# The gate's activations of a recurrence with a highway layer: u stored as pairs of tokens and transposed as 32-bit words

## The chip, the cores and the metric

The kernel runs on one core of a Trainium2 chip. The metric is the device time of one execution in microseconds, of which the median over several runs is given. The times of the profile come from one profiled execution; its span goes from the first to the last instruction.

## What is computed

The input is x and f_logit, both 4 x 6336 x 256 in float32, a lower bound and a bias of 256 values each, and two matrices of 256 x 256. The first half is a recurrence over the 6336 tokens of each of four batches, the second a highway layer on its output:

```python
sig = 1.0 / (1.0 + np.exp(-f_logit))
f = lower_bound + (1.0 - lower_bound) * sig
i = 1.0 - f
for t in range(S):
    h = f[:, t] * h + i[:, t] * x[:, t]
    y[:, t] = h
H = np.maximum(y @ w_h, 0.0)
T = 1.0 / (1.0 + np.exp(-(y @ w_t + b_t)))
out = T * H + (1.0 - T) * y
```

## The kernel before

The 25344 tokens are cut into 29 units. A full unit has 1024 tokens of one batch: partition p of 128 holds 8 neighbouring tokens (nb = 8) with their 256 channels. Three units at the start and three at the end are shorter (2 or 4 tokens a partition), and one has 6 tokens a partition from four batches. A unit goes through these stages, each a function whose letter stands in the order:

- l and x load f_logit and x (tokens on the partitions), on the SP queue.
- u (L240) is one ScalarE instruction: u = sigmoid(-f_logit), which is 1 - sig, stored as f16 in the tile `u`.
- b (L246) multiplies u with x, two tokens of each partition in one instruction, on GpSimd or, where the order says v, on VectorE. The result `bv` is bf16 and is stored as pairs: the values of two neighbouring tokens lie side by side for each channel.
- i (L255) transposes u on TensorE, for one half h of the channels, to channels on the partitions: one transpose of 128 x 128 f16 for each of the nb tokens. It goes into one PSUM bank, `uT`, where the tokens then lie sorted by j, the place of a token within its partition.
- f (L263) computes f = 1 - (1 - lower_bound) u from uT, on ScalarE or (v) VectorE. It reads uT in steps, so that the tokens come in their order, and stores f16 in order.
- p (L279) transposes bv, for one half of the channels, with one f32 transpose for each pair of tokens: two bf16 values make one 32-bit word. The words are written in steps of nb/2 words, so that `bT` has the tokens in order.
- s (L301) is the recurrence, one scan on VectorE along the tokens, from f and bT to `y`, with the last column of the unit before as its start.
- z and g (L312) are the two matrix products, t (L328) the sigmoid of z on ScalarE, d (L333) the maximum with g on VectorE, E and e (L339) the product of d and t on GpSimd and VectorE.
- o (L350) brings tokens back to the partitions on TensorE (`op`), c (L365) copies it to SBUF on ScalarE, and w stores it through SP.

The channel factor 1 - lower_bound, by which b leaves out a part of i, is multiplied into the weights and into `diag` once at the start.

The order of all of this is a list written out in the kernel (L72 to L123); each word is a stage with its unit, its half and, behind a colon, its PSUM slot. uT and bT share two slots of one bank each (a0 and a1), and z, g and op share three slots of two banks (b0 to b2). Every instruction is pinned to the order of the list on its engine. The helper `shared` (L209) makes a product on GpSimd wait for the product on VectorE ahead of it in the list.

Of the kernel before, what the change touches and what calls it, by code (L numbers as in the profile page):

```python
# [11 lines left out]
FP32 = mybir.dt.float32  # L12
BF16 = mybir.dt.bfloat16
FP16 = mybir.dt.float16
AF = mybir.ActivationFunctionType
# [4 lines left out]
def kernel(  # L20
# [10 lines left out]
    nc = tc.nc  # L31
    B, S, D = x.shape
    assert (B, S, D) == (4, 6336, 256)
    P = 128
    NH = D // P
    NB = 8
# [3 lines left out]
    units = [  # L40
        (0, 128, 2, 0, 'y', 4, 0),
        (0, 128, 2, 256, 'y', 4, 0),
        (0, 128, 4, 512, 'y', 4, 0),
        (0, 128, 8, 1024, 'y', 4, 1280),
        (0, 128, 8, 2048, 'y', 4, 2048),
        (0, 128, 8, 3072, 'y', 4, 0),
        (0, 128, 8, 4096, 'y', 4, 2048),
        (0, 128, 8, 5120, 'yk', 4, 0),
# [81 lines left out]
    st = [dict() for _ in range(NU)]  # L130
    pin = tc.keep_in_program_order

    def sb(shape, dtype, name):
        return pool.tile(shape, dtype, tag=name, name=name, bufs=bufs.get(name, 1))

    def one_bank(slot, dtype, name):
        return ps.tile([P, NB * P], dtype, tag=f"a{slot}", name=name)
# [7 lines left out]
    ident_h = sb([P, P], FP16, "ident_h")  # L145
    make_identity(nc, ident_h)
    ident_f = sb([P, P], FP32, "ident_f")
# [21 lines left out]
    def tokens(n):  # L169
        return units[n][1] * units[n][2]  # L170
# [38 lines left out]
    def shared(ins, gpsimd):  # L209

        if not gpsimd:
            held[:] = [ins]
        elif held:
            tc.add_manual_dep(ins.ins, held.pop().ins.name, mybir.DependencyInfo(
                mybir.DependencyClass.Sync, mybir.DependencyReason.DATA), reason="shared port")
# [23 lines left out]

    def do_u(n, k, eng, slot):  # L240
        np_, nb = units[n][1:3]
        u = sb([P, NB, D], FP16, "u")
        pin(nc.scalar.activation(u[:np_, :nb], st[n]["l"][:np_, :nb], AF.Sigmoid, scale=-1.0))  # L243
        st[n]["u"] = u

    def do_b(n, k, eng, slot):  # L246
        np_ = units[n][1]
        if "bv" not in st[n]:
            st[n]["bv"] = sb([P, NB // 2, D, 2], BF16, "bv")
        q = 2 * k  # L250
        e = nc.vector if eng else nc.gpsimd
        shared(pin(e.tensor_mul(st[n]["bv"][:np_, k].rearrange("p d j -> p j d"), st[n]["u"][:np_, q:q + 2],  # L252
                                st[n]["x"][:np_, q:q + 2])), not eng)

    def do_i(n, h, eng, slot):  # L255
        np_, nb = units[n][1:3]
        uT = one_bank(slot, FP16, "uT")
        for j in range(nb):
            pin(nc.tensor.transpose(uT[:, j * np_:(j + 1) * np_], st[n]["u"][:np_, j, h * P:(h + 1) * P],  # L259
                                    ident_h[:np_, :np_]))  # L260
        st[n]["uT", h] = uT

    def do_f(n, h, eng, slot):  # L263
        N, nb = tokens(n), units[n][2]
        f = sb([P, NB * P], FP16, "f")
        to, of = f[:, :N], st[n]["uT", h][:, :N]
        if isinstance(units[n][0], int):
            to = to.rearrange("c (p j) -> c p j", j=nb)
            of = of.rearrange("c (j p) -> c p j", j=nb)
        else:  # L270
            to = to.rearrange("c (b p j) -> c b p j", b=B, j=nb)
            of = of.rearrange("c (j p b) -> c b p j", b=B, j=nb)
        if eng:
            pin(nc.vector.tensor_scalar(to, of, ncc[:, h:h + 1], 1.0, op0=ALU.mult, op1=ALU.add))
        else:
            pin(nc.scalar.activation(to, of, AF.Identity, scale=ncc[:, h:h + 1], bias=1.0))  # L276
        st[n]["f", h] = f

    def do_p(n, h, eng, slot):  # L279
        np_, nb = units[n][1:3]  # L280
        bT = one_bank(slot, BF16, "bT")
        words = bT.bitcast(FP32)
        g = nb // 2
        for k in range(g):
            pair = st[n]["bv"][:np_, k, h * P:(h + 1) * P].rearrange("p d j -> p (d j)").bitcast(FP32)
            if isinstance(units[n][0], int):
                to = words[:, k:k + g * (np_ - 1) + 1:g]
            else:
                to = words[:, :g * np_].rearrange("c (b p k) -> c p b k", b=B, k=g)[:, :, :, k]
            pin(nc.tensor.transpose(to, pair, ident_f[:np_, :np_]))  # L290
        st[n]["bT", h] = bT

    carry = {}
# [88 lines left out]
    for token in order.split():  # L382
# [5 lines left out]
        n, _, k = name[1:].partition(".")  # L388
# [29 lines left out]
```

## Time and profile before

| | |
|---|---|
| runs of the kernel, device us | 218.88 median of 3 (216.72 to 220.64) |
| span of the profiled execution | 215.2 us |
| TensorE (PE) busy | 190.1 us, 88% |
| VectorE (DVE) busy | 199.2 us, 93% |
| ScalarE (ACT) busy | 195.9 us, 91% |
| GpSimd (POOL) busy | 178.9 us, 83% |
| granted TensorE clock | 0.999 |
| moved by DMA | 78.69 MB, 366 GB/s in the mean |

The profiled execution has no device time of its own on record, only its span; the runs are 1.5 to 5.4 us longer than that span, which counts from the first instruction to the last. PE is the line of the matmuls and PEld that of the weight loads, which overlap them. A group of the profile gives the line, the engine, the operation, the tiles (result <- inputs) with partitions x elements and type, the count, the busy time in us and the mean of one in ns, and then the idle time of the engine just before them with what ended it.

### The profile page before, as it was taken

How to read it: one execution, taken by the hardware profiler on the slowest of the kernel's cores; microseconds unless marked ns; L12 is line 12 of the kernel's file. 1: busy time of each engine (PE TensorE's matmuls, PEld its weight loads, DVE VectorE, ACT ScalarE, POOL GpSimd, SP SyncE). 2: the span in 40 equal slices, each digit the busy share in tenths (PEclk: the TensorE clock that was granted, in tenths of full speed). 3: DMA queues.
4: the chain of work that ended last, by engine and by line, in shares of the span. 5: the costliest groups of instructions: out<-in, count | busy, mean ns of one | idle time of the engine just before them, and what ended most of it. 6: DMA issues, size and time to landing. Idle time of an engine off the chain costs nothing. (4 is left out here: it accounts for less than half of the span.)

```text
span 215.2 us, 4648 instructions
## 1 busy us (share of the span) xinstructions
PE 190.1 (88%) x1784; PEld 132.4 (62%) x1811; DVE 199.2 (93%) x164; ACT 195.9 (91%) x195; POOL 178.9 (83%) x166
## 2 busy tenths in 40 slices
PE   7477778988999799999998999999899999999881
PEld 3144456655766666675676766667676576776661
DVE  2789998999999899999998999999999999999960
ACT  4579889999999999999999999999999999999772
POOL 3045789997999999899998999887988999898910
PEclk9999999999999999999999999999999999999999
DMA  6999999999999999999999799998999999498275
GB/s 185 395 420 417 423 419 410 423 316 315 429 416 425 411 426 393 350 411 414 428 425 416 324 329 326 431 399 287 330 412 420 419 422 420 165 321 360 110 285 200
DMA packets 16750, 78.69 MB, mean 366 GB/s; under 512 B 2004, under 2 KB 2776, under 8 KB 11096
## 3 DMA queue, kind: packets, MB, share of 16 engines
q1 hardware_dynamic: 16720, 78.39, 92.7%
q8 instruction: 14, 0.23, 0.4%
q14 instruction: 8, 0.07, 0.1%
q10 hardware_dynamic: 8, 0.00, 0.0%
HBM read 52.43 MB, written 25.95 MB: 364 GB/s over the span
## 5 line engine op out<-in xcount | busy, mean ns | idle before, releaser
L252 POOL TENSOR_TENSOR bv<-u,x 128x512 bf16<-128x512 f16 x95 | 112.8, 1217 | 21.7 <-DVE w_sb L197 9.0
L307 DVE TENSOR_TENSOR_SCAN y<-f,y,bT 128x1024 bf16<-128x1024 f16 (+2 forms) x46 | 92.8, 2032 | 1.6 <-ACT f L276 0.9
L342 POOL TENSOR_TENSOR e<-d,t 128x512 bf16<-128x512 bf16 (+1 forms) x60 | 67.7, 1148 | 3.9 <-DVE e L342 3.0
L336 DVE SCALAR_TENSOR_TENSOR d<-y,ncc,g 128x1024 bf16<-128x1024 bf16 (+2 forms) x54 | 58.9, 1101 | 2.4 <-PE g L318 2.3
L331 ACT ACTIVATE t<-z,bt 128x1024 bf16<-128x1024 f32 (+3 forms) x58 | 57.9, 1019 | 2.0 <-PE z L318 1.3
L276 ACT ACTIVATE f<-uT,ncc 128x1024 f16<-128x1024 f16 (+3 forms) x53 | 55.4, 1057 | 4.2 <-PE uT L259 2.8
L318 PEld LDWEIGHTS <-w_sb 128*128 128x128 f16 x416 | 39.3, 99 | 32.2 <-issue 2.7
L372 ACT COPY o<-op 128x1024 f32<-128x1024 f32 (+2 forms) x53 | 51.2, 983 | 4.7 <-PE op L362 3.1
L243 ACT ACTIVATE u<-l 128x2048 f16<-128x2048 f32 (+3 forms) x29 | 49.2, 1695 | 3.8 <-DMA l<-in_f_logit_dram 3.6
L362 PE MATMUL op<-ident_b,e 128*128 128x128 bf16 x396 | 49.4, 219 | 1.0 <-DVE e L342 0.8
L318 PE MATMUL z<-y,w_sb 128*128 128x512 bf16 (+1 forms) x179 | 47.5, 372 | 1.2 <-DVE d L336 0.2
L318 PE MATMUL g<-y,w_sb 128*128 128x512 bf16 (+1 forms) x181 | 47.9, 372 | 0.7
L362 PEld LDWEIGHTS <-e 128*128 128x128 bf16 x396 | 44.0, 113 | 5.7 <-issue 2.2
L361 PE MATMUL op<-diag,y 128*128 128x128 f16 x368 | 45.9, 219 | 1.6 <-ACT o L372 0.9
L361 PEld LDWEIGHTS <-y 128*128 128x128 bf16 x368 | 41.0, 113 | 1.9
L290 PE MATMUL bT<-ident_f,bv 128*128 128x128 f32 x198 | 33.6, 283 | 7.2 <-POOL bv L252 2.5
L259 PE MATMUL uT<-ident_h,u 128*128 128x128 f16 x396 | 31.9, 221 | 7.7 <-DVE y L307 2.5
L259 PEld LDWEIGHTS <-u 128*128 128x128 f16 x396 | 26.6, 99 | 18.5 <-issue 7.9
L290 PEld LDWEIGHTS bT<-ident_f,bv 128*128 128x128 f32 x198 | 23.1, 142 | 17.0 <-POOL bv L252 3.8
L342 DVE TENSOR_TENSOR e<-d,t 128x512 bf16<-128x512 bf16 (+5 forms) x19 | 17.7, 943 | 1.0 <-PE op L362 0.7
L307 DVE TENSOR_TENSOR_SCAN y<-f,yr,bT 128x1024 bf16<-128x1024 f16 x4 | 9.3, 2333 | 0.0
L252 DVE TENSOR_TENSOR bv<-u,x 128x512 bf16<-128x512 f16 x4 | 3.4, 855 | 3.1 <-DMA x<-in_x_dram 3.1
(42 smaller groups left out, 48.9 us busy)
## 6 DMA issues: line engine op xcount, KB each, us to landing
out_dram<-o SPq DMA_DIRECT2D x46, 512.0 KB, 7.7
l<-in_f_logit_dram SPq DMA_DIRECT2D x22, 1024.0 KB, 11.1
x<-in_x_dram SPq DMA_DIRECT2D x22, 1024.0 KB, 13.8
l<-in_f_logit_dram SPq DMA_DIRECT2D x4, 256.0 KB, 8.7
x<-in_x_dram SPq DMA_DIRECT2D x4, 256.0 KB, 4.5
l<-in_f_logit_dram SPq DMA_DIRECT2D x2, 512.0 KB, 9.7
x<-in_x_dram SPq DMA_DIRECT2D x2, 512.0 KB, 7.5
out_dram<-o SPq DMA_DIRECT2D x3, 256.0 KB, 13.9
```

The source lines that it names most:

```text
L252: shared(pin(e.tensor_mul(st[n]["bv"][:np_, k].rearrange("p d j -> p j d"), st[n]["u"][:np_, q:q + 2], st[n]["x"][:np_, q:q + 2])), not eng)
L259: pin(nc.tensor.transpose(uT[:, j * np_:(j + 1) * np_], st[n]["u"][:np_, j, h * P:(h + 1) * P], ident_h[:np_, :np_]))
L276: pin(nc.scalar.activation(to, of, AF.Identity, scale=ncc[:, h:h + 1], bias=1.0))
L290: pin(nc.tensor.transpose(to, pair, ident_f[:np_, :np_]))
L307: pin(nc.vector.tensor_tensor_scan(y[:, c0:c0 + ln], st[n]["f", h][:, c0:c0 + ln], st[n]["bT", h][:, c0:c0 + ln], 0.0 if prev is None else ...
L318: pin(nc.tensor.matmul(p[:, a:e], w_sb[:, k, ki, m * P:(m + 1) * P], half(n, "y", ki)[:, a:e], start=ki == 0, stop=ki == NH - 1))
L331: pin(nc.scalar.activation(half(n, "t", m), st[n]["z", m][:, :tokens(n)], AF.Sigmoid, bias=bt[:, m:m + 1]))
L336: pin(nc.vector.scalar_tensor_tensor(half(n, "d", m), half(n, "y", m), ncc[:, m:m + 1], st[n]["g", m][:, :tokens(n)], op0=ALU.mult, op1=AL ...
L342: shared(pin(eng.tensor_mul(st[n]["e"][:, a:e], st[n]["d"][:, a:e], st[n]["t"][:, a:e])), eng is nc.gpsimd)
L361: pin(nc.tensor.matmul(o, half(n, "y", h)[:, cols], diag[:, h], start=True, stop=False))
L362: pin(nc.tensor.matmul(o, half(n, "e", h)[:, cols], ident_b, start=False, stop=True))
L372: pin(nc.scalar.copy(o[:np_, :w], st[n]["op", q][:np_, :w]))
```

## The change

The tile u gets the layout of bv: for each pair k of neighbouring tokens and each channel d, the two values lie side by side. ScalarE's one instruction for u stays one instruction and stores each f16 value 4 bytes from the one before it. The product b reads u in that layout. The stage i uses what p did: one f32 transpose for each pair of tokens and half, written in steps into the bank, through a common function `pairs`; p calls the same function. Then uT has the tokens in order, and f reads it in order, without the rearranged view. The list of the order, the slots, the tiles' sizes and the counts of instructions on ScalarE, VectorE, GpSimd and SP stay as they are; the transposes of u become half as many.

```diff
     def do_u(n, k, eng, slot):
         np_, nb = units[n][1:3]
-        u = sb([P, NB, D], FP16, "u")
-        pin(nc.scalar.activation(u[:np_, :nb], st[n]["l"][:np_, :nb], AF.Sigmoid, scale=-1.0))
+        u = sb([P, NB // 2, D, 2], FP16, "u")
+        pin(nc.scalar.activation(u[:np_, :nb // 2].rearrange("p k d j -> p k j d"),
+                                 st[n]["l"][:np_, :nb].rearrange("p (k j) d -> p k j d", j=2), AF.Sigmoid, scale=-1.0))
...
-        shared(pin(e.tensor_mul(st[n]["bv"][:np_, k].rearrange("p d j -> p j d"), st[n]["u"][:np_, q:q + 2],
-                                st[n]["x"][:np_, q:q + 2])), not eng)
+        shared(pin(e.tensor_mul(st[n]["bv"][:np_, k].rearrange("p d j -> p j d"),
+                                st[n]["u"][:np_, k].rearrange("p d j -> p j d"), st[n]["x"][:np_, q:q + 2])), not eng)
+
+    def pairs(n, src, h, words):
+        np_, g = units[n][1], units[n][2] // 2
+        for k in range(g):
+            pair = src[:np_, k, h * P:(h + 1) * P].rearrange("p d j -> p (d j)").bitcast(FP32)
+            if isinstance(units[n][0], int):
+                to = words[:, k:k + g * (np_ - 1) + 1:g]
+            else:
+                to = words[:, :g * np_].rearrange("c (b p k) -> c p b k", b=B, k=g)[:, :, :, k]
+            pin(nc.tensor.transpose(to, pair, ident_f[:np_, :np_]))
...
     def do_i(n, h, eng, slot):
-        np_, nb = units[n][1:3]
         uT = one_bank(slot, FP16, "uT")
-        for j in range(nb):
-            pin(nc.tensor.transpose(uT[:, j * np_:(j + 1) * np_], st[n]["u"][:np_, j, h * P:(h + 1) * P],
-                                    ident_h[:np_, :np_]))
+        pairs(n, st[n]["u"], h, uT.bitcast(FP32))
         st[n]["uT", h] = uT
...
         to, of = f[:, :N], st[n]["uT", h][:, :N]
-        if isinstance(units[n][0], int):
-            to = to.rearrange("c (p j) -> c p j", j=nb)
-            of = of.rearrange("c (j p) -> c p j", j=nb)
-        else:
-            to = to.rearrange("c (b p j) -> c b p j", b=B, j=nb)
-            of = of.rearrange("c (j p b) -> c b p j", b=B, j=nb)
...
     def do_p(n, h, eng, slot):
...
+        pairs(n, st[n]["bv"], h, bT.bitcast(FP32))
         st[n]["bT", h] = bT
```

More of the change, by code (lines that the diff above doesn't have):

```diff
@@ L251, in do_b @@
         e = nc.vector if eng else nc.gpsimd
-        shared(pin(e.tensor_mul(st[n]["bv"][:np_, k].rearrange("p d j -> p j d"), st[n]["u"][:np_, q:q + 2],
-                                st[n]["x"][:np_, q:q + 2])), not eng)
+        shared(pin(e.tensor_mul(st[n]["bv"][:np_, k].rearrange("p d j -> p j d"),
[9 more added lines that the diff above has]
+            pin(nc.tensor.transpose(to, pair, ident_f[:np_, :np_]))
     def do_i(n, h, eng, slot):
-        np_, nb = units[n][1:3]
         uT = one_bank(slot, FP16, "uT")
-        for j in range(nb):
-            pin(nc.tensor.transpose(uT[:, j * np_:(j + 1) * np_], st[n]["u"][:np_, j, h * P:(h + 1) * P],
-                                    ident_h[:np_, :np_]))
+        pairs(n, st[n]["u"], h, uT.bitcast(FP32))
         st[n]["uT", h] = uT
     def do_f(n, h, eng, slot):
-        N, nb = tokens(n), units[n][2]
+        N = tokens(n)
         f = sb([P, NB * P], FP16, "f")
         to, of = f[:, :N], st[n]["uT", h][:, :N]
-        if isinstance(units[n][0], int):
-            to = to.rearrange("c (p j) -> c p j", j=nb)
-            of = of.rearrange("c (j p) -> c p j", j=nb)
-        else:
-            to = to.rearrange("c (b p j) -> c b p j", b=B, j=nb)
-            of = of.rearrange("c (j p b) -> c b p j", b=B, j=nb)
         if eng:
@@ L279, in do_p @@
     def do_p(n, h, eng, slot):
-        np_, nb = units[n][1:3]
         bT = one_bank(slot, BF16, "bT")
[L282 to L290, printed above, removed]
+        pairs(n, st[n]["bv"], h, bT.bitcast(FP32))
         st[n]["bT", h] = bT
```

## The prediction

> **What bounds the kernel now.** I read the busy times first, then the windows, then the groups of equal shape, and last PE's line of time around a few transposes.
>
> The page's first part has four engines near their limit:
>
> ```profile
> PE 190.1 (88%) x1784; PEld 132.4 (62%) x1811; DVE 199.2 (93%) x164; ACT 195.9 (91%) x195; POOL 178.9 (83%) x166
> ```
>
> A share of the whole span mixes a ramp, a body and a tail, so the body is read by itself: nine windows of 20 us. The columns are the busy us of PE, PEld, DVE, ACT and POOL, then the clock, the DMA share and GB/s.
>
> ```profile
> 20.00:40.00 20.00, 16.58 (x153) 11.28 (x154) 19.25 (x15) 18.38 (x18) 16.77 (x16) 1.00 1.01 419
> 40.00:60.00 20.00, 18.17 (x167) 12.51 (x169) 20.00 (x13) 19.99 (x19) 18.48 (x16) 1.00 0.98 364
> 60.00:80.00 20.00, 17.88 (x175) 12.71 (x177) 18.87 (x12) 18.89 (x19) 19.73 (x18) 1.00 1.02 422
> 80.00:100.00 20.00, 19.41 (x189) 13.79 (x190) 20.00 (x15) 19.47 (x19) 18.94 (x17) 1.00 1.01 390
> 100.00:120.00 20.00, 18.53 (x167) 12.60 (x170) 19.37 (x20) 20.00 (x19) 19.24 (x19) 1.00 1.02 422
> 120.00:140.00 20.00, 18.99 (x191) 13.54 (x190) 20.00 (x12) 19.67 (x20) 18.81 (x17) 1.00 0.93 347
> 140.00:160.00 20.00, 18.74 (x211) 14.45 (x212) 19.97 (x13) 19.55 (x19) 18.12 (x16) 1.00 0.96 355
> 160.00:180.00 20.00, 19.39 (x177) 13.12 (x178) 20.00 (x14) 19.40 (x19) 18.87 (x17) 1.00 1.02 418
> 180.00:200.00 20.00, 19.79 (x196) 14.22 (x199) 20.00 (x16) 19.03 (x22) 18.11 (x17) 1.00 0.75 290
> ```
>
> Added up from 20 to 200 us: DVE is busy 177.5 of 180 us, ACT 174.4, POOL 167.1. DVE sets the pace of the body; it has 2.5 us of idle time to give. ACT can become 3.1 us slower before it has as little slack as DVE, and POOL 10.4 us. So what the change does to DVE counts nearly in full, what it does to ACT counts after about 3 us, what it does to POOL after about 10.
>
> **The change, part by part.** The order of instructions on ACT, DVE, POOL and SP is the same before and after; no DMA, no slot and no queue position moves. Only PE has fewer instructions. What can change is how long single instructions take. The rows for that, by shape (busy us, mean ns), and two rows with least, median and greatest ns of one:
>
> ```profile
> L331 ACT ACTIVATE t<-z,bt 128x1024 bf16<-128x1024 f32 x44 | 49.7, 1150 | 0.9 <-PE z L318 0.5 <-POOL e L342 0.4
> L276 ACT ACTIVATE f<-uT,ncc 128x1024 f16<-128x1024 f16 x43 | 49.3, 1158 | 1.6 <-PE uT L259 1.6
> L372 ACT COPY o<-op 128x1024 f32<-128x1024 f32 x47 | 48.3, 1044 | 3.7 <-PE op L362 2.5 <-ACT f L276 0.4 <-DMA out_dram<-o 0.4
> L243 ACT ACTIVATE u<-l 128x2048 f16<-128x2048 f32 x22 | 42.9, 1952 | 1.3 <-DMA l<-in_f_logit_dram 1.2
> L342 POOL TENSOR_TENSOR e<-d,t 128x512 bf16<-128x512 bf16 x55 | 63.9, 1181 | 2.1 <-DVE e L342 1.2 <-PE uT L259 0.8
> L252 POOL TENSOR_TENSOR bv<-u,x x95: 1160/1178/2191, 11.3 to 203.5; 128x512 bf16<-128x512 f16 x95
> L252 DVE TENSOR_TENSOR bv<-u,x x4: 720/732/1236, 4.2 to 18.4; 128x512 bf16<-128x512 f16 x4
> L336 DVE SCALAR_TENSOR_TENSOR d<-y,ncc,g 128x512 bf16<-128x512 bf16 x4 | 2.8, 728 | 0.0
> L274 DVE TENSOR_SCALAR f<-uT,ncc 128x1024 f16<-128x1024 f16 x1 | 1.3, 1279 | 0.0
> L342 DVE TENSOR_TENSOR e<-d,t 128x1024 bf16<-128x1024 bf16 x5 | 3.7, 746 | 0.0
> ```
>
> *PE: 396 f16 transposes become 198 f32 ones.* The f32 kind is already there as bT, so it has a price. From PE's line of time (start, us, group):
>
> ```profile
> 162.82 0.61 PE L259 MATMUL uT<-ident_h,u 128*128 128x128 f16 x8
> 163.27 1.03 PE L318 MATMUL z<-y,w_sb 128*128 128x512 bf16 x4
> 164.13 0.60 PE L290 MATMUL bT<-ident_f,bv 128*128 128x128 f32 x4
> 164.57 0.22 PE L361 MATMUL op<-diag,y 128*128 128x128 f16 x1
> ```
>
> Eight f16 transposes hold PE from 162.82 to 163.27, 0.45 us, and end 0.61 us after their start; four f32 ones hold it from 164.13 to 164.57, 0.44 us, and end after 0.60 us. Half as many instructions, each twice as long: 198 x 0.11 us for 396 x 0.056 us, 22 us either way. I take 0. What could differ is the start after a wait, because an f16 weight load is a separate instruction that may go ahead of the wait. The bT group at 178.61 us, which came after a wait, took 0.63 us; that bounds the loss near 0.03 us for each of 58 stages, 1.7 us if every one lay on the path. The chain of waits gives uT 1.2% of the span, so I take +0.1 us.
>
> The writes into PSUM become scattered: uT was written packed, and will be written in steps of 16 bytes (for units of 8 tokens a partition), as bT is. By the rows above that costs nothing: bT, written in these steps, holds PE 0.44 us for what uT does packed in 0.45 us. [...]
>
> *ACT f (53 times) reads in order and no longer in steps of 256 bytes.* f at 1158 ns stands beside t at 1150 ns, which reads f32 in order. The gather costs 8 ns at most by that row, 0.4 us in 53; the far bound is o with 1044 ns (no per-partition operand), 114 ns x 53 = 6 us. I take t, which has an operand of that kind too. ACT is not the tightest engine, so of 0.4 us I count -0.1.
>
> *ACT u (29 times) stores f16 in steps of 4 bytes.* No ACT instruction of the trace stores so. From below: f16 packed (f, 1158) and bf16 packed (t, 1150) go at one pace, and f32 stores of o, whose elements lie 4 bytes apart, are no slower; ACT seems to go by the element. On POOL a bv instruction, which stores in such steps and reads a wider x, has a median of 1178 ns (its mean, 1217, is drawn up by a few slow ones) where the mean e has 1181. [...] From above: DVE's packed e needs 551 ns for 512 elements in the mean and bv 732, so 0.35 ns an element more where a packed pace is lost; u has 50688 elements a partition in all (25344 tokens x 256 / 128), so 18 us. I take 0, since ACT shows no packed pace that could be lost.
>
> *POOL bv (95 times) and DVE bv (4) read u in steps of 4 bytes.* x, f32, is read in such steps already beside u, and e with both inputs packed in 16 bits is no faster. I take 0; from above, each POOL instruction costs about 2.2 ns an element, and if the step made u's read a third as dear again as the whole, 0.7 ns, this would be 95 x 512 x 0.7 ns = 34 us, less POOL's 10.4 us of slack. DVE's four lie in the ramp.
>
> *DVE f (5 times).* In order, 16 bits in and out, DVE may find a pace of two elements: e of 1024 elements takes 746 ns, f 1279. That bounds the gain by 0.53 us for the one of 1024, some 0.26 us for that of 512 and 0.13 us for each of three of 256: 1.2 us. But f's source is PSUM, e's is not; the one of 1024 lies in the body, where DVE counts. From below 0. I take -0.3 us.
>
> *Sum:* +0.1 - 0.1 + 0 + 0 - 0.3 = -0.3 us on the profiled execution's span of 215.2 us. The median of the runs, 218.88 us, lies 3.7 us above that span (the runs shown range from 1.5 to 5.4 us above it); nothing in the change touches what lies around the span. So 218.88 - 0.3 = 218.6 us.
>
> **The rivals.**
>
> *A: the strided store costs ACT (slower).* Place: the 29 u instructions. For it: no row shows this store on ACT. Against it: the two other engines do it for 4 ns or less. It decides once u's sum grows by ACT's 3.1 us of slack, 6% of u's 49.2 us; 2% on the clock needs 3.1 + 4.4 = 7.5 us, 15%. At the far bound of 18 us: 218.9 + 18 - 3.1 = 234 us.
>
> *B: POOL's read of u in steps costs (slower).* Place: bv, and after it p, the scan and DVE. For it: POOL's two inputs would both come in steps of 4 bytes, which no row has. Against it: bv, with one such input and such a store, is level with e. It decides from 10.4 us, 0.11 us for each bv; at the far bound 218.9 + 34 - 10.4 = 242 us.
>
> *C: the change relieves more than one instruction (faster).* If f fell to o's 1044 ns, ACT would win 6 us, and DVE its 1.2 us; f would be ready earlier and some of DVE's 2.5 us of idle time in the body would close. All of it: 218.9 - 1.2 - 2.5 = 215.2 us; with a little of the ramp (DVE is busy 13.8 of the first 20 us) 214. Against it: f and t are level, and PE's work is the same.
>
> *D: small shifts change who waits for whom.* Four engines with little slack in a fixed order can lose or win a few us through a stall that moves (in the list of waits POOL's bv waited 6 times for x, 7.8 us together). Nothing sizes it; it is the width of the forecast: 215 to 223 us.
>
> *E: scattered writes slow the f32 transposes of u (slower).* If they went at half of bT's pace, PE would be busy 198 x 0.11 = 22 us longer; PE is busy 167.5 of the 180 us of the body, 10.0 us more idle than DVE, so 218.9 + 22 - 10 = 231 us. It decides from those 10 us. Against it: bT's pace. [...]
>
> **How the numbers follow.** Forecast with D inside 2%: 0.57. A 0.13, B 0.09, C 0.15, D slower by more than 2% 0.05, E 0.01. So faster by over 2% 0.15, within 2% 0.57, slower 0.28; 2%, 4.4 us, is about what a measurement of this kernel can tell from no change, as its three runs lie 1.8% apart. The forecast's own range is 215 to 223. The range of 8 in 10 reaches to a part of C and to mild cases of A and B, where the store or the read costs some 10 us and the slack is taken off: 213.8 to 226.0. Only their far bounds are left out.
>
> **What would show it.** Right: the f32 uT groups of four hold PE 0.44 us; u of 2048 elements stays within 30 ns of 1952; f between 1140 and 1160; POOL bv at a median near 1178; DVE at 20.0 in most windows of the body. Step by step wrong: u above 2200 ns is A; bv above 1300 ns is B; f near 1050 ns, or DVE's f of 1024 near 750 ns, is C; uT groups of four above 0.5 us would undo the PE row. The prediction as a whole is wrong if any engine's row moves by over 10%, or if the time leaves 214.5 to 223.3 us with all rows unchanged.

## The result, and the profile after

The change makes the kernel slower: 225.38 us median of 4 runs (224.27 to 225.49) against 217.84 us for the kernel before (4 runs), a ratio of 1.033 with a 95% interval from 1.028 to 1.037. The forecast was 218.6 us, no change. The measured time is what the forecast listed as rival A, a store of u that costs ScalarE, at a chance of 0.13. The range, to 226.0 us, still holds it. In the experiments below, times and ratios leave out the few executions over 1.5% longer than the fastest of their kernel; the profiled executions of e6 and e10 were such, so their spans and waits are not compared.

First the page's busy times of the changed kernel, span 223.7 us (before 215.2 us):

```profile
PE 192.9 (86%) x1589; PEld 133.5 (60%) x1613; DVE 202.3 (90%) x164; ACT 208.8 (93%) x195; POOL 188.4 (84%) x166
```

ACT gained 12.9 us and POOL 9.5 us; DVE gained 3.1 us, PE 2.8 us. ACT is now the busiest engine. Six of the nine windows (busy us of PE, PEld, DVE, ACT, POOL, then clock, DMA share, GB/s) show it better:

```profile
40.00:60.00 20.00, 16.50 (x121) 10.39 (x122) 19.60 (x13) 20.00 (x16) 19.22 (x16) 1.00 0.83 300
60.00:80.00 20.00, 17.73 (x169) 13.35 (x173) 17.94 (x11) 20.00 (x18) 18.15 (x15) 1.00 1.01 414
80.00:100.00 20.00, 18.99 (x162) 13.00 (x162) 19.96 (x14) 19.99 (x19) 19.38 (x17) 1.00 1.00 374
120.00:140.00 20.00, 17.43 (x157) 12.12 (x158) 18.69 (x12) 20.00 (x19) 18.38 (x16) 1.00 0.74 263
140.00:160.00 20.00, 18.63 (x148) 12.76 (x151) 19.52 (x13) 20.00 (x19) 17.72 (x16) 1.00 0.96 364
160.00:180.00 20.00, 18.55 (x174) 13.53 (x175) 20.00 (x13) 20.00 (x19) 19.35 (x18) 1.00 1.01 403
```

ACT is idle for 0.01 us in these six windows together, and DVE, which set the pace before, has holes of up to 2.1 us. Over all nine windows, from 20 to 200 us, ACT is busy 179.2 of 180 us (before 174.4) and DVE 172.0 (before 177.5). The places have changed. The lists of waits show by which way (us in total, times, longest); first the kernel before, then the changed one:

```profile
PE uT L259 <- ACT f L276: 2.4, 5, 0.8
DVE y L307 <- PE bT L290: 0.7, 1, 0.7
```

```profile
PE uT L264 <- ACT f L278: 5.8, 9, 1.2
DVE y L300 <- PE bT L264: 2.3, 5, 0.6
```

TensorE waits longer for ScalarE, whose f frees the slot that the next transposes need, and VectorE's scan waits longer for TensorE's bT.

The groups by shape, and the least, median and greatest ns of the product, say where ACT's and POOL's time comes from:

```profile
L243 ACT ACTIVATE u<-l 128x2048 f16<-128x2048 f32 x22 | 57.7, 2623 | 0.0
L324 ACT ACTIVATE t<-z,bt 128x1024 bf16<-128x1024 f32 x44 | 51.2, 1192 | 0.1
L278 ACT ACTIVATE f<-uT,ncc 128x1024 f16<-128x1024 f16 x43 | 50.5, 1194 | 1.8 <-PE uT L264 1.7
L253 POOL TENSOR_TENSOR bv<-u,x x95: 1257/1281/2279, 11.6 to 212.3; 128x512 bf16<-128x512 f16 x95
L276 DVE TENSOR_SCALAR f<-uT,ncc 128x1024 f16<-128x1024 f16 x1 | 0.7, 741 | 0.0
```

u of 2048 elements went from 1952 to 2623 ns, 34% more; all 29 u together from 49.2 to 65.6 us, 16.4 us more. f reads in order and is no cheaper on ACT: f and t stand level, as before. That f, t and o each rose by 36 to 46 ns, though only f was touched, goes with an ACT that hardly pauses: in e5 below, with u stored as before and ACT nearly as busy, they rose by 25 to 35 ns and u to 1979 ns. Against that u, the stride costs 644 ns. POOL's product went from a median of 1178 to 1281 ns. The one f of 1024 on DVE fell from 1279 to 741 ns. ACT's busy time grew by less than u's group, since the records of instructions that follow each other closely overlap: in the kernel before, the groups t, f, o and u add up to 213.7 us where ACT is busy for 195.9, and in the changed one to 233.8 where it is busy for 208.8.

And PE, a stretch of its line of time (start, us, group):

```profile
188.22 0.60 PE L264 MATMUL bT<-ident_f,bv 128*128 128x128 f32 x4
188.66 0.60 PE L264 MATMUL uT<-ident_f,u 128*128 128x128 f32 x4
189.09 1.03 PE L311 MATMUL z<-y,w_sb 128*128 128x512 bf16 x4
```

Four f32 transposes of u hold PE from 188.66 to 189.09, 0.43 us, just as those of bv do.

### The profile page after: what moved, and what is told of

It is laid out like the page before. It is cut to its first block, busy times and chain, and to the rows that moved or that the text cites. A ratio compares the mean times of both kernels' runs of the same rounds, so it can differ in the third digit from the quotient of the medians.

```text
span 223.7 us, 4262 instructions
## 1 busy us (share of the span) xinstructions
PE 192.9 (86%) x1589; PEld 133.5 (60%) x1613; DVE 202.3 (90%) x164; ACT 208.8 (93%) x195; POOL 188.4 (84%) x166
## 4 chain that ended last, share of the span: by engine, by line
PE 34%; ACT 30%; DVE 11%; issue 11%; POOL 6%; DMA 3%; POOLq 1%; SPq 1%; ACTq 0%; DVEq 0%
PE z L311 10%; ACT f L278 8%; ACT t L324 8%; ACT u L243 8%; DVE y L300 7%; PE g L311 6%; PE uT L264 6%; ACT o L365 6%; POOL bv L253 4%; PE bT L264 4%; PE op L355 4%; PE op L354 4%; DMA l<-in_f_logit_dram 3%; DVE d L329 3%; POOL e L335 2%
## 5 line engine op out<-in xcount | busy, mean ns | idle before, releaser
L253 POOL TENSOR_TENSOR bv<-u,x 128x512 bf16<-128x512 f16 x95 | 122.0, 1310 | 19.3 <-DVE w_sb L197 9.3
L243 ACT ACTIVATE u<-l 128x2048 f16<-128x2048 f32 (+3 forms) x29 | 65.6, 2263 | 2.9 <-DMA l<-in_f_logit_dram 2.9
L311 PEld LDWEIGHTS <-w_sb 128*128 128x128 f16 x416 | 41.0, 100 | 38.6 <-issue 9.2
L278 ACT ACTIVATE f<-uT,ncc 128x1024 f16<-128x1024 f16 (+3 forms) x53 | 56.6, 1087 | 4.1 <-PE uT L264 3.1
L324 ACT ACTIVATE t<-z,bt 128x1024 bf16<-128x1024 f32 (+3 forms) x58 | 59.4, 1051 | 1.0 <-PE z L311 0.7
L365 ACT COPY o<-op 128x1024 f32<-128x1024 f32 (+2 forms) x53 | 52.2, 1028 | 2.4 <-PE op L355 1.9
L264 PE MATMUL uT<-ident_f,u 128*128 128x128 f32 x198 | 33.7, 289 | 10.9 <-ACT f L278 5.8
L264 PEld LDWEIGHTS uT<-ident_f,u 128*128 128x128 f32 x198 | 23.7, 145 | 22.3 <-ACT f L278 9.5
L335 DVE TENSOR_TENSOR e<-d,t 128x512 bf16<-128x512 bf16 (+5 forms) x19 | 20.9, 1111 | 1.0 <-ACT t L324 0.6
L300 DVE TENSOR_TENSOR_SCAN y<-f,bT 128x256 bf16<-128x256 f16 (+1 forms) x4 | 5.9, 1485 | 0.8 <-ACT f L278 0.4
```

The costliest lines, as they stand in the source:

```text
L243: pin(nc.scalar.activation(u[:np_, :nb // 2].rearrange("p k d j -> p k j d"), st[n]["l"][:np_, :nb].rearrange("p (k j) d -> p k j d", j=2) ...
L300: pin(nc.vector.tensor_tensor_scan(y[:, c0:c0 + ln], st[n]["f", h][:, c0:c0 + ln], st[n]["bT", h][:, c0:c0 + ln], 0.0 if prev is None else ...
L311: pin(nc.tensor.matmul(p[:, a:e], w_sb[:, k, ki, m * P:(m + 1) * P], half(n, "y", ki)[:, a:e], start=ki == 0, stop=ki == NH - 1))
L324: pin(nc.scalar.activation(half(n, "t", m), st[n]["z", m][:, :tokens(n)], AF.Sigmoid, bias=bt[:, m:m + 1]))
L335: shared(pin(eng.tensor_mul(st[n]["e"][:, a:e], st[n]["d"][:, a:e], st[n]["t"][:, a:e])), eng is nc.gpsimd)
L365: pin(nc.scalar.copy(o[:np_, :w], st[n]["op", q][:np_, :w]))
```

## Experiments

The theory after the result, A: ScalarE's store of f16 values in steps of 4 bytes is slow in itself, ScalarE becomes the bound, and this is the loss. Rival B: GpSimd's slower read. Rival P: the f32 transposes, with a lower granted clock (0.967 in the profiled execution, 0.69 in its first 20 us). Their weight loads wait with them: in the changed kernel those of u wait 9.5 us for ACT's f, while the f16 loads before show no wait for it, though their transposes wait 2.4 us for it on PE. Ratios are to the kernel before on the same chip, with 95% intervals.

| run | what differs from the kernel before | us | ratio | span, ACT busy |
|---|---|---|---|---|
| before | | 217.8 | 1 | 215.2, 195.9 |
| after | all of the change | 225.4 | 1.033 [1.028, 1.037] | 223.7, 208.8 |
| e1_layout_only | strided store and read, old transposes | 225.6 | 1.037 [1.031, 1.043] | 222.7, 209.0 |
| e9_store_only | strided store | 225.8 | 1.040 [1.035, 1.045] | 223.1, 208.6 |
| e10_read_only | strided read by the product | 220.7 | 1.016 [1.011, 1.022] | |
| e6_transposes_only | f32 transposes, f in order | 214.7 | 0.989 [0.984, 0.994] | |
| e7_f_in_order | f in order | 217.6 | 0.999 [0.995, 1.002] | 214.4, 195.5 |
| e5_more_scalar_time | more packed ScalarE work | 223.5 | 1.027 [1.021, 1.034] | 220.4, 207.7 |
| e2_packed_store | after, ScalarE reads in jumps instead | 222.3 | 1.023 [1.015, 1.031] | 220.5, 206.1 |
| e3_packed_product | e2, product packed too | 220.5 | 1.016 [1.010, 1.021] | 218.8, 206.0 |
| e12_f_to_vector | e3, six f on VectorE | 222.8 | 1.024 [1.019, 1.029] | 221.7, 201.5 |

A span is from one execution, the time is a median.

### The layout without the transposes

e1_layout_only:

```diff
 # the kernel before, with u stored in pairs and the product reading pairs, as in the change, and
-            pin(nc.tensor.transpose(uT[:, j * np_:(j + 1) * np_], st[n]["u"][:np_, j, h * P:(h + 1) * P],
+            pin(nc.tensor.transpose(uT[:, j * np_:(j + 1) * np_], st[n]["u"][:np_, j // 2, h * P:(h + 1) * P, j % 2],
```

> u is stored and read as pairs, but the 396 f16 transposes and the gathered read of f stay as in the kernel before. Theory A (ScalarE's store of u in steps of 4 bytes, 16.4 us more busy time in u, makes ScalarE the bound): nearly the whole loss is here, 224 to 227 us, u of 2048 elements near 2600 ns. Rival P (the f32 transposes of u, which cannot load weights ahead of a wait, and the lower TensorE clock): the loss is gone, near 218 us.

Measured: 225.56 us, u of 2048 elements 2634 ns. The whole loss is here without a single new transpose. (The old transposes read u in steps of 4 bytes here; at 222 ns in the mean they stand level with 221 before.) In its profiled execution the granted clock is 0.998 and the span still 222.7 us, so the clock is not the cause either. Rival P falls.

### Store and read apart

e9_store_only stores in pairs and lets everything else read the bytes packed; e10_read_only stores packed and lets the product read in steps:

```diff
 # e9
-        pin(nc.scalar.activation(u[:np_, :nb], st[n]["l"][:np_, :nb], AF.Sigmoid, scale=-1.0))
+        pr = u.rearrange("p n d -> p (n d)").rearrange("p (k d j) -> p k j d", d=D, j=2)
+        pin(nc.scalar.activation(pr[:np_, :nb // 2],
+                                 st[n]["l"][:np_, :nb].rearrange("p (k j) d -> p k j d", j=2), AF.Sigmoid, scale=-1.0))
 # e10
-        st[n]["u"][:np_, q:q + 2],
+        st[n]["u"].rearrange("p n d -> p (n d)").rearrange("p (k d j) -> p k j d", d=D, j=2)[:np_, k],
```

> The kernel before with ScalarE's store of u alone in steps of 4 bytes; product and transposes read the same bytes packed, so the sorting of u's values is left out. Theory A: u of 2048 elements near 2620 ns, the product at 1180 ns, and most of the loss, 223 to 225.5 us. Rival B: 220 us or less.

> The kernel before with the product's read of u alone in steps of 4 bytes; the store is packed, so the sorting of u's values is left out for the product. Theory A: the product rises to about 1280 ns, but GpSimd has slack, and the time stays within 1.5 us of before. Rival B: 221 us or more. If both this and e9_store_only lose, and the two losses add up to more or less than that of e1_layout_only (8 us), the two are not independent.

The groups by shape of e9 and, behind them, of e10:

```profile
L244 ACT ACTIVATE u<-l 128x2048 f16<-128x2048 f32 x22 | 57.7, 2621 | 0.0
L254 POOL TENSOR_TENSOR bv<-u,x 128x512 bf16<-128x512 f16 x95 | 112.0, 1204 | 26.7 <-ACT f L278 10.3 <-ACT u L244 8.5 <-DVE e L344 3.8
```

```profile
L243 ACT ACTIVATE u<-l 128x2048 f16<-128x2048 f32 x22 | 42.5, 1932 | 0.1
L252 POOL TENSOR_TENSOR bv<-u,x 128x512 bf16<-128x512 f16 x95 | 121.7, 1308 | 17.5 <-DVE w_sb L197 9.4 <-DMA x<-in_x_dram 3.0 <-ACT u L243 2.3
```

The store alone makes u 2621 ns, leaves the product at 1204 ns in the mean, and loses 4.0%, all of the change's loss. The read alone makes the product slower by the same 0.1 us as in the changed kernel and loses 1.6%, though A allowed it nothing beyond 1.5 us: 3.5 us were lost (1.6% of 216.9), so A missed here, and B's 221 us was not quite reached. The two add up to 5.6%, and e1 with both lost 3.7%: they are not independent, and where the store is strided already, the strided read adds no loss that can be measured.

Why a GpSimd with idle time costs anything stays open. A likely way is the transposes of bv: in the kernel before, PE waits 2.5 us, in 5 waits, for GpSimd's bv, so a product that ends later can hold up the transpose and with it the scan. The traces that can be compared do not settle it: PE's wait for bv is 2.1 us in e1, with the slower product, and 1.8 us in e9, without it.

### ScalarE's time without the stride

e5_more_scalar_time:

```diff
         pin(nc.scalar.activation(u[:np_, :nb], st[n]["l"][:np_, :nb], AF.Sigmoid, scale=-1.0))
+        m = 64 * nb
+        pin(nc.scalar.activation(more[:np_, :m], st[n]["l"][:np_, :nb].rearrange("p j d -> p (j d)")[:, :m],
+                                 AF.Sigmoid, scale=-1.0))
```

> The kernel before, and behind each u one more packed instruction on ScalarE over a quarter of u's elements, stored in a tile that nobody reads; about 16 us of ScalarE time in all, nothing else changed. Theory A: 223 to 228 us, as the changed kernel. Rivals B and P: ScalarE's time alone does not make the loss; 220 us or less.

The groups of u and of the added work by shape:

```profile
L244 ACT ACTIVATE u<-l 128x2048 f16<-128x2048 f32 x22 | 43.5, 1979 | 0.5 <-DMA l<-in_f_logit_dram 0.4
L246 ACT ACTIVATE more<-l 128x512 f16<-128x512 f32 x22 | 15.2, 692 | 0.0
```

Measured: 223.52 us. Packed work of 17.8 us (15.2 us of it in the 22 full units) and nothing else loses 2.7%. ScalarE's time alone makes most of a loss of this size. The last column of the table says it in another way: in after, e1, e9, e5, e2 and e3 the span is ACT's busy time and 12.7 to 14.9 us more. Before, it was 19.3 us more, in e7 18.9, and in e12, with six f less on ScalarE, 20.2.

### The transposes and the order of f alone

e6_transposes_only is the changed kernel with u stored and multiplied in token order; e7_f_in_order is the kernel before with only f's rearranged views gone:

```diff
 # e6, against the changed kernel
+        tok = u.rearrange("p k d j -> p (k d j)").rearrange("p (n d) -> p n d", d=D)
-        pin(nc.scalar.activation(u[:np_, :nb // 2].rearrange("p k d j -> p k j d"),
-                                 st[n]["l"][:np_, :nb].rearrange("p (k j) d -> p k j d", j=2), AF.Sigmoid, scale=-1.0))
+        pin(nc.scalar.activation(tok[:np_, :nb], st[n]["l"][:np_, :nb], AF.Sigmoid, scale=-1.0))
 # e7, against the kernel before
-            to = to.rearrange("c (p j) -> c p j", j=nb)
-            of = of.rearrange("c (j p) -> c p j", j=nb)
```

> The f32 transposes and the in-order read of f of the changed kernel, but ScalarE stores u packed in token order and the product reads it so; a 32-bit word then holds two neighbouring channels of one token in place of two tokens of one channel, which leaves out the right sorting of u's transpose. Counts, shapes and steps of the transposes and of f are those of the changed kernel. Theory A: no loss, 0 to 1 us faster than before (216.5 to 218 us), since only VectorE's five f get cheaper. Rival P: 2 us or more slower than before.

> The kernel before, f16 transposes and all, but f reads uT in the order in which it lies, so f's tokens stay sorted by their place within the partition and the scan pairs them wrongly. Only the read of f differs. If the 1.1% that e6_transposes_only won come from VectorE's five f (1.2 us together, one element packed pace), this wins 0.5% or so; if they come from the f32 transposes, this wins nothing.

e6 wins 1.1%, and e7, with VectorE's f of 1024 elements at 743 ns, wins nothing that can be measured. A had expected 216.5 to 218 us of e6, which was faster than that. So the f32 transposes are a small gain, 2.4 us together with f's order, where the forecast had a loss of 0.1, and the cheaper f on VectorE, put at 0.3 us, is worth nothing visible. What is left between the two is the transposes: 198 f32 ones with scattered writes in place of 396 f16 ones with packed writes, at equal time on PE (0.43 us for four in the changed kernel, 0.45 for eight before). Which part of that is worth the gain was not tried.

### Single instructions, with nothing beside them

The kernel of the run micro has, behind all units, rows of single instructions:

```diff
+    for _ in range(6):   # L400: f16 packed
+        pin(nc.scalar.activation(b16[:, :1024], src[:, :1024], AF.Sigmoid, scale=-1.0))
+    for _ in range(6):   # L402: f16 in steps of 4 bytes
+        pin(nc.scalar.activation(b16[:, 0:2048:2], src[:, :1024], AF.Sigmoid, scale=-1.0))
+    for _ in range(6):   # L404: f16 in steps of 8 bytes
+        pin(nc.scalar.activation(b16[:, 0:4096:4], src[:, :1024], AF.Sigmoid, scale=-1.0))
...
```

> The kernel before, and behind all its units rows of single instructions, each some times in a row, with nothing else running: ScalarE from 1024 f32 elements to f16 packed, in steps of 4 and 8 bytes, in pairs, packed with the read in jumps, to f32 packed and in steps of 8 bytes, and with a read in steps of 8 bytes; the product of 512 elements on GpSimd and on VectorE in the five layouts of the experiments; f from PSUM in order and gathered on ScalarE and VectorE. Theory A, told by the element: store in steps of 4 bytes some 300 ns above packed, even without load from elsewhere. If the store costs nothing here, the loss in the kernel comes from contention. A store of f32 packed at the packed f16 pace would show that it is not the 4 bytes between elements but the half-filled word that costs.

ScalarE's groups, each 1024 elements (L406 is the store of the changed kernel, L408 packed with a read in jumps, L410 f32 packed, L412 f32 in steps of 8 bytes, L414 a read in steps of 8 bytes):

```profile
L404 ACT ACTIVATE x<-l 128x1024 f16<-128x1024 f32 x6 | 14.8, 2472 | 0.2
L402 ACT ACTIVATE x<-l 128x1024 f16<-128x1024 f32 x6 | 8.0, 1335 | 0.2
L406 ACT ACTIVATE x<-l 128x1024 f16<-128x1024 f32 x6 | 8.0, 1335 | 0.2
L408 ACT ACTIVATE x<-l 128x1024 f16<-128x1024 f32 x6 | 7.7, 1278 | 0.2
L412 ACT ACTIVATE x<-l 128x1024 f32<-128x1024 f32 x6 | 6.7, 1115 | 0.2
L414 ACT ACTIVATE x<-l 128x1024 f16<-128x1024 f32 x6 | 6.6, 1107 | 0.2
L400 ACT ACTIVATE x<-l 128x1024 f16<-128x1024 f32 x6 | 6.3, 1056 | 3.1 <-DVE x L395 2.9
L410 ACT ACTIVATE x<-l 128x1024 f32<-128x1024 f32 x6 | 6.3, 1056 | 0.2
```

Without any load from elsewhere, in one execution, the store in steps of 4 bytes costs 279 ns in 1024 elements, 0.27 ns each. Not the distance makes it: f32 values, 4 bytes apart by nature, go at the pace of packed f16, and f32 in steps of 8 bytes costs 59 ns. f16 in steps of 8 bytes takes 2472 ns. So on ScalarE the scattered 16-bit stores took 279 and 1416 ns more than packed ones, where the 32-bit stores over the same bytes took 0 and 59 ns more. In the kernel the price was larger, 671 ns for 2048 elements, 0.33 ns each, or 644 ns against e5's u.

The other engines, GpSimd's product with u packed (L427, the kernel before) and in steps (L429, the change), the same two on VectorE, and f on ScalarE and VectorE in order (L442, L446) and gathered (L444, L448):

```profile
L429 POOL TENSOR_TENSOR bv<-u,l 128x512 bf16<-128x512 f16 x5 | 6.3, 1267 | 0.4
L427 POOL TENSOR_TENSOR bv<-u,l 128x512 bf16<-128x512 f16 x5 | 5.8, 1163 | 78.0 <-ACT u L416 77.7
L433 POOL TENSOR_TENSOR bv<-u,l 128x512 bf16<-128x512 f16 x5 | 5.8, 1155 | 0.4
L442 ACT ACTIVATE f<-uT,ncc 128x1024 f16<-128x1024 f16 x5 | 5.6, 1114 | 1.3 <-PE uT L438 1.1
L444 ACT ACTIVATE f<-uT,ncc 128x1024 f16<-128x1024 f16 x5 | 5.6, 1114 | 0.2
L446 DVE TENSOR_SCALAR f<-uT,ncc 128x1024 f16<-128x1024 f16 x5 | 3.7, 749 | 0.1
L448 DVE TENSOR_SCALAR f<-uT,ncc 128x1024 f16<-128x1024 f16 x5 | 6.4, 1284 | 0.2
L427 DVE TENSOR_TENSOR bv<-u,l 128x512 bf16<-128x512 f16 x5 | 3.6, 729 | 100.4 <-POOL bv L435 100.2
L429 DVE TENSOR_TENSOR bv<-u,l 128x512 bf16<-128x512 f16 x5 | 3.6, 727 | 0.2
L433 DVE TENSOR_TENSOR bv<-u,l 128x512 bf16<-128x512 f16 x5 | 3.5, 693 | 0.2
```

On GpSimd a 16-bit read in steps costs 104 ns, while the scattered 16-bit store of bv, against all packed (L433), costs 8. VectorE does not mind the read (729 and 727 ns); the scattered store costs it 36 ns against all packed (693). The gather from PSUM costs ScalarE nothing, 1114 ns both ways; VectorE pays 535 ns for it.

### Other ways to the same layout

e2_packed_store lets ScalarE go through u in the order of its storage; e3_packed_product does the same in the product; e12_f_to_vector then moves six f to VectorE:

```diff
 # e2, against the changed kernel
-        pin(nc.scalar.activation(u[:np_, :nb // 2].rearrange("p k d j -> p k j d"),
-                                 st[n]["l"][:np_, :nb].rearrange("p (k j) d -> p k j d", j=2), AF.Sigmoid, scale=-1.0))
+        pin(nc.scalar.activation(u[:np_, :nb // 2],
+                                 st[n]["l"][:np_, :nb].rearrange("p (k j) d -> p k d j", j=2), AF.Sigmoid, scale=-1.0))
 # e3, against e2
-        shared(pin(e.tensor_mul(st[n]["bv"][:np_, k].rearrange("p d j -> p j d"),
-                                st[n]["u"][:np_, k].rearrange("p d j -> p j d"), st[n]["x"][:np_, q:q + 2])), not eng)
+        shared(pin(e.tensor_mul(st[n]["bv"][:np_, k],
+                                st[n]["u"][:np_, k], st[n]["x"][:np_, q:q + 2].rearrange("p j d -> p d j"))), not eng)
 # e12, against e3: in the order
-f6.1 f9.0 f12.0 f17.0 f20.0 f22.1
+f6.1v f9.0v f12.0v f17.0v f20.0v f22.1v
```

> The changed kernel, but ScalarE goes through u in the order of its storage, so it stores packed and reads f_logit in jumps of 1024 bytes between the two tokens of a pair. Theory A: u of 2048 elements falls back to about 1950 ns if the read in jumps is free, and the time to 217 to 220 us. Rival B (GpSimd reading u in steps of 4 bytes, 103 ns more for each of 95 products): GpSimd stays at 1280 ns and the time at 222 us or more. Rival P: the time stays near 225 us.

> As e2_packed_store, and the product too goes through its tiles in the order of storage: u read packed, bv stored packed, x read in jumps of 1024 bytes. Theory A: no difference to e2_packed_store beyond 2 us, whatever GpSimd does within its slack. Rival B: if the product returns to 1180 ns or below, the time falls by several us against e2_packed_store; if jumps on x cost GpSimd more, it rises.

> As e3_packed_product, and six f of 1024 elements (f6.1, f9.0, f12.0, f17.0, f20.0, f22.1) go from ScalarE to VectorE, where a read in order takes about 745 ns. Theory A: with ScalarE as the bound, 6 x 1.1 = 6.6 us off ScalarE and 4.5 us onto VectorE win 1 to 4 us against e3_packed_product (220.5 us), which would be level with the kernel before, 217 to 219 us. If VectorE is as tight, nothing is won.

e2: u takes 2458 ns, since the read in jumps of 1024 bytes costs nearly as much as the store in steps (222 against 279 ns in the quiet row), and the time 222.3 us. A's hope that the read in jumps is free was wrong, and B had foretold 222 us or more, so e2 by itself does not tell A from B. e3: the product falls from a median of 1283 to 1234 ns, and the time to 220.5 us; the intervals of e2 and e3 overlap, so that part is not settled. e12 is no faster than e3, 222.8 us: six f less on ScalarE did not pay. ScalarE's busy time fell from 206.0 to 201.5 us and VectorE's rose from 200.1 to 203.5; that VectorE is now as tight is the likely reason, but no run shows it. No version with the right sorting beats the kernel before; e6 is faster, but its words hold two channels where f needs two tokens.

## Why the prediction was wrong

*The step that failed: "ACT u ... I take 0, since ACT shows no packed pace that could be lost".* Its working stood on ScalarE's f16 and f32 stores going at one pace, which the quiet rows confirm (1056 ns both), and on GpSimd and VectorE storing 16-bit values in steps for 4 ns or less, which holds roughly (8 ns on GpSimd, 36 ns on VectorE, in 512 elements). What did not follow is that ScalarE does so as well: 279 ns in 1024 elements quiet, 671 ns in 2048 in the kernel. The sign named for A, u above 2200 ns, came. The far bound, 18 us, lay near the 16.4 us measured, but by luck: it was worked out from VectorE's 551 and 732 ns for e and bv, and the quiet rows show ScalarE at one pace for packed f16 and f32. When no row of the engine itself shows an access, two other engines are no proof for it.

*The 0 for POOL bv failed too*: 103 ns for each product, 9.8 us in all. The comparison of bv with e could not show it, because x was f32 in steps of 4 bytes (bv 1178 ns, e 1181), and what costs is a 16-bit value in such steps: 1267 ns against 1163 in the quiet rows, 9%.

*The slack of the windows was half right.* For ScalarE it held in kind: 12.9 us more busy time became 8.5 us of span, 4.4 us were absorbed, where 3.1 were counted. Rival A's formula, fed with u's own 16.4 us, would have given 218.9 + 16.4 - 3.1 = 232 us, 6.8 above the 225.4 measured. The overlap of the records takes 3.5 us of that (12.9 in place of 16.4) and the larger slack 1.3; the other 2 are the 3.7 us that the forecast put between span and run, where each run whose own span is on record lies 1.7 to 1.9 us above it. For GpSimd, 10.4 us of slack were counted and the loss came anyway, 3.5 us in e10: idle time summed over a window does not say whether the product that someone waits for ends later.

*Right:* PE's row (four f32 transposes hold PE 0.43 us against 0.44 forecast), so rival E falls; whether f32 transposes written packed would be faster still, no run shows; ACT's gather of f costs nothing; VectorE's f gains 538 ns at 1024 elements (1279 to 741), the bound of 0.53 us. *Right in size, wrong in worth:* that last gain, the sign named for C, which e7 cannot show in the time, and the f32 transposes, where 0.1 us of loss were put and e6 won 1.1%. The 1.2% of the span for uT, on which that 0.1 us leaned, came from a chain that was followed back only to 139.62 us.

## What to carry to other kernels

Before a tile's layout is changed for a later reader, price the writer on its own engine: here 22 us of transposes stayed as they were, while the store that made the layout cost 16.4 us on an engine that had 3 to spare. In every form tried here the 16-bit interleave was paid somewhere, by a store or a read in steps or in jumps; put it on the engine for which a quiet row of single instructions shows it free and which is not the bound. And do not take an engine's idle time, summed over a window, as an allowance: GpSimd's 10.4 us did not absorb 95 products that each took 0.1 us longer.

## What the runs showed of the hardware

On ScalarE, f16 stores of 1024 elements took 1056 ns packed, 1335 ns in steps of 4 bytes and 2472 ns in steps of 8, while f32 stores took 1056 and, in steps of 8 bytes, 1115 ns. Reading f32 from SBUF in steps of 8 bytes took 1107 ns, in jumps of 1024 bytes between two rows 1278. On GpSimd an f16 input in steps of 4 bytes costs 104 ns in 512 elements and a bf16 output in such steps 8; on VectorE the two cost nothing and 36. VectorE's f from PSUM runs at 749 ns in order and 1284 gathered; ScalarE's at 1114 both ways.
